# Block attention with a soft mixture of experts: units of 512 tokens by one head pair, quarter-array transposes, v on GpSimd's queue, one arena, full-width w2 and result

## The chip, the cores and the metric

One core of a Trainium2 chip runs the whole program. The metric is device time in microseconds (us) of one execution; three runs of the kernel before are given, and one profiled execution of it. PE is TensorE, DVE is VectorE, ACT is ScalarE, POOL is GpSimd, and SP is the sync engine, which computes nothing here and issues DMAs. A q behind an engine's name means its queue of such instructions.

## The reference, cut to what matters

```python
# attention inside chunks of 64 tokens; B, H, S, D = 8, 8, 576, 64
scores = (q_c @ k_c.T) / sqrt(D)                  # 64 x 64 for each chunk and head
attn = softmax(scores)                            # with 1e-9 in the denominator
x = (attn @ v_c) -> rows of tokens                # N = 4608 tokens, 512 columns: 8 heads of 64
# soft mixture of experts: 8 experts with 4 slots each
logits = x @ phi                                  # 4608 x 32
d = softmax(logits over the tokens);  c = softmax(logits over the slots)
slot_in = d.T @ x                                 # 32 x 512
slot_out[e] = relu(slot_in[e] @ w1[e]) @ w2[e]    # w1: 512 x 1024, w2: 1024 x 512, e = 0..7
out = c @ slot_out                                # 4608 x 512
```

All is float32. The program reads 9.4 MB each of q, k and v and 16.8 MB each of w1 and w2, and writes 9.4 MB.

## The kernel before

**Attention** works on 36 tiles `t` of 128 tokens, that is two chunks of all eight heads. `load_qk` brings 128 tokens of q and of k, with eight tokens of one head (2 KB of DRAM) on each partition; where the two chunks belong to different sequences it takes two DMAs of 1 KB rows each. `load_v` brings v in four DMAs of 64 KB with rows of 256 bytes, from POOL's queue for the first four tiles and from SP's for all others. `transposes` turns q or k with four transposes of the whole 128x128 array (L153, results `pq` and `pk`), and four copies sort each into `qT` and the block-diagonal `kT_bd` (L176 on DVE, L178 on ACT). `s1` makes the scores `psc` (L191) and subtracts the maximum; `s1b` is the exponential; `s2a` transposes the weights (`pt`, L214); `s2b` multiplies by v (`pav`, L231) and divides; `s3` transposes x (`px`, L252). Once in four tiles `logits` (`pl`, L267), `natural` (`pe`) and `partial` (`pp`, L337) carry the softmax over the tokens on.

**Order.** Each engine runs its instructions in the order in which the code issues them; the loop over `t` is written as a software pipeline by hand. One turn of it issues `load_qk(t + 3)`, `load_v(t)`, sometimes a load of 1 MB of w1 (`load_w`), and then on PE: `psc` of tile t, the transposes of t+2, `px` of t-3, `pt` of t-1 and `pav` of t-2. A DMA on SP's queue waits there until its buffer is free, and what stands behind it waits too. There are four buffers for q and k together and three for v.

**Experts.** `up` (`ph`, L549) multiplies the slots by w1, two experts at a time, `turn` transposes the result, and `down` (`po`, L579) multiplies by w2. w2 comes in halves of the columns, in rows of 1 KB: first the left columns of all experts, then the right ones. So the left half of the result can be formed (`pf`, L614, in one-pass float32r with weights that `place_c` has split in two) and written, in rows of 1 KB, while the right columns of w2 still come in.

```python
            if t + 3 < NT:
                load_qk(t + 3)
            load_v(t)
            ...
            s1(t)
            ...
            if t + 2 < NT:
                transposes(t + 2, 1)
                transposes(t + 2, 0)
```

Of the kernel before, what the change touches and what calls it, by code (L numbers as in the profile page):

```python
# [9 lines left out]
F32R = mybir.dt.float32r  # L10
# [6 lines left out]
def kernel(  # L17
# [17 lines left out]
    NC = S // CH                 # chunks per sequence  # L35
# [4 lines left out]
    NT = N // P                  # 128-token tiles, two chunks each  # L40
    PT = P // H                  # partitions per head of a loaded tile
    JT = P // PT                 # tokens per partition of a loaded tile
    J2 = JT // 2
    NL = NT // 4                 # logit batches of four tiles
    E, _, FF = w1.shape
    SL = phi.shape[1]            # slots
# [4 lines left out]
    NWA = 17  # L51
    NWB = 5
    NV = 3
    NQK = 4
    NK = 2

    const = ctx.enter_context(tc.tile_pool(name="const", bufs=1))
    wpa = ctx.enter_context(tc.tile_pool(name="wpa", bufs=NWA))
# [4 lines left out]
    c_all = const.tile([P, NT, SL], F32, name="c_all")  # L63
# [15 lines left out]
    DH = DM // 2  # L79
    wt = {}  # L80
    worder = [(1, e, h) for e in range(E) for h in range(2)]
    worder += [(2, e, h) for h in range(2) for e in range(E)]

    def load_w(pool, n):
        m, e, h = worder[n]
        t = pool.tile([P, 2048], F32, tag="w", name=f"w{m}_{e}_{h}") if pool else qk_w
        if m == 1:
            t = t.rearrange("p (j f) -> p j f", j=2)
            nc.sync.dma_start(t, w1[e].rearrange("(j p) f -> p j f", p=P)[:, 2 * h:2 * h + 2])
        else:  # L90
            t = t.rearrange("p (g f) -> p g f", g=8)
            nc.sync.dma_start(
                t, w2[e].rearrange("(g p) f -> p g f", p=P)[:, :, DH * h:DH * (h + 1)])
        wt[m, e, h] = t

    with ExitStack() as actx:
        ap_ = actx.enter_context(tc.tile_pool(name="attn1", bufs=1))
        asc = actx.enter_context(tc.tile_pool(name="attn_sc", bufs=2))
        av_ = actx.enter_context(tc.tile_pool(name="attn_v", bufs=1))
        a2 = actx.enter_context(tc.tile_pool(name="attn2", bufs=2))  # L100
        ps = actx.enter_context(tc.tile_pool(name="ps", bufs=8, space=PSUM))
# [12 lines left out]
        qTb = [ap_.tile([P, NHP, P], F32, name=f"qT{i}") for i in range(2)]  # L114
        kT_bd = [ap_.tile([P, 2, NHP, P], F32, name="kT_bd0")]
        xT = av_.tile([P, 4, NF, P], F32, name="xT")
        v_bd = [av_.tile([P, 2, NHP, VW], F32, name=f"v_bd{i}") for i in reversed(range(NV))][::-1]
        kT_bd.append(av_.tile([P, 2, NHP, P], F32, name="kT_bd1"))

        def chunk(t, c2):  # L120
            b, c = divmod(2 * t + c2, NC)
            return b, c * CH

        def load_qk(t):
            (b0, s0), (b1, s1_) = chunk(t, 0), chunk(t, 1)
            for src, dst in ((k, qkn[2 * t % NQK]), (q, qkn[(2 * t + 1) % NQK])):
                if b0 == b1:
                    nc.sync.dma_start(
                        dst.rearrange("p j d -> p (j d)"),
                        src[b0][:, s0:s0 + P].rearrange("h (p j) d -> p h (j d)", j=JT),  # L130
                    )
                else:
                    for c2, (b, s0_) in enumerate(((b0, s0), (b1, s1_))):
                        nc.sync.dma_start(
                            dst[:, J2 * c2:J2 * (c2 + 1), :].rearrange("p j d -> p (j d)"),
                            src[b][:, s0_:s0_ + CH].rearrange("h (p j) d -> p h (j d)", j=J2),
                        )

        def load_v(t):
            for c2 in range(2):  # L140
                b, s0 = chunk(t, c2)
                for a in range(2):
                    (nc.gpsimd if t < 4 else nc.sync).dma_start(
                        v_bd[t % NV][CH * a:CH * (a + 1), c2, :, (D + 1) * a:(D + 1) * a + D],
                        v[b, a::2, s0:s0 + CH].rearrange("hp x d -> x hp d"),
                    )

        def transposes(t, isk):
            src = qkn[(2 * t + 1 - isk) % NQK]
            dst = kT_bd[t % NK] if isk else qTb[t % 2]  # L150
            pt = bank(f"p{'qk'[isk]}_{t}")
            for i in range(J2):
                nc.tensor.transpose(  # L153
                    out=pt[:, P * i:P * (i + 1)],
                    in_=src[:, 2 * i:2 * i + 2, :].rearrange("x u d -> x (u d)"),
                    identity=ident,
                )
            pv = pt.rearrange("x (j p hp a) -> x a hp p j", j=J2, a=2, p=PT)
            split = chunk(t, 0)[0] != chunk(t, 1)[0]
            for u in range(2):  # L160
                for a in range(2):
                    r = slice(D * a, D * (a + 1))
                    d = dst[r, a] if isk else dst[r]
                    s = pv[D * u:D * (u + 1), a]
                    pieces = []
                    if not split:
                        pieces.append((d.rearrange("x hp (p j u) -> x u hp p j", j=J2, u=2)[:, u], s))
                    else:
                        J4 = J2 // 2
# [12 lines left out]
        def s1(t):
            psc = bank(f"psc_{t}")
            qT, kb = qTb[t % 2], kT_bd[t % NK]
            for c2 in range(2):
                cs = slice(CH * c2, CH * (c2 + 1))
                for hp2 in range(2):
                    for hpg in range(2):
                        hp = 2 * hpg + hp2
                        o = (c2 * 2 + hp2) * P  # L190
                        nc.tensor.matmul(  # L191
                            psc[CH * hpg:CH * (hpg + 1), o:o + P],
                            lhsT=qT[:, hp, cs],
                            rhs=kb[:, :, hp, cs],
                            start=True, stop=True,
                        )
            pv = psc.rearrange("p (r x) -> p r x", x=CH)
            mx = a2.tile([P, 8], F32, tag="mx", name=f"mx_{t}")
            nc.vector.reduce_max(mx, pv, axis=AX.X)  # L199
            sc = asc.tile([P, 8, CH], F32, tag="sc", name=f"sc_{t}")  # L200
            nc.vector.tensor_tensor(sc, pv, mx.unsqueeze(2).to_broadcast([P, 8, CH]), ALU.subtract)  # L201
            ex[t] = sc

        def s1b(t):
            nc.scalar.activation(ex[t], ex[t], AF.Exp, scale=SCALE)  # L205

        xs = {}
        ats = {}

        def s2a(t):  # L210
            sc = ex.pop(t).rearrange("p (r h) x -> p r (h x)", h=2)
            pt = bank(f"pt_{t}")
            for r in range(4):
                nc.tensor.transpose(out=pt[:, P * r:P * (r + 1)], in_=sc[:, r], identity=ident)  # L214
# [466 lines left out]
```

## Time and profile before

| | |
|---|---|
| three runs | 282.5, 283.17 and 284.31 us, median 283.17 us |
| profiled execution | span 284.7 us from its first to its last instruction; no separate time is given for it |
| PE, DVE, ACT, POOL busy | 236.2, 182.0, 169.6, 20.3 us |
| DMA | 71.83 MB in 77906 packets, mean 252 GB/s; SP's queue 94.3% of 16 engines' span |
| chain that ended last | PE 46%, DMA 42%, DVE 4%, ACT 2% |
| attention | first `psc` at 8.54 us, that of the last tile at 201.10 us |
| experts | first `ph` at 220.63 us |

A profile row gives an engine's busy time in a stretch, or one merged group of instructions with its start, its length and its count. One float32 matmul stands as two records on PE, a transpose as one. DMA share is the mean busy share of the 16 DMA engines; it can exceed 1 since packets overlap.

### The profile page before, as it was taken

The numbers are of one execution on the slowest core, as the hardware profiler recorded it, in microseconds if no ns is written. First come the engines' busy times: TensorE is split into PE (matmuls) and PEld (weight loads), VectorE is DVE, ScalarE is ACT, GpSimd is POOL, SyncE is SP. The second block draws the span as 40 slices with busy tenths as digits, with TensorE's granted clock in tenths as the row PEclk, the third lists the DMA queues.
The fourth block names the chain that finished last, engine by engine and source line by source line (L and its number), as shares of the span: only waits on it lengthen the run. The fifth ranks groups of instructions, "written<-read, shape, count | busy, mean of one in ns | idle before, by whom it ended". The sixth has DMA issues, their size and how long they took to land.

```text
span 284.7 us, 7167 instructions
## 1 busy us (share of the span) xinstructions
PE 236.2 (83%) x2629; PEld 180.3 (63%) x2629; DVE 182.0 (64%) x504; ACT 169.6 (60%) x429; POOL 20.3 (7%) x53
## 2 busy tenths in 40 slices
PE   6869978978798988768997698696899999999850
PEld 3648867767586677557785567575676235677850
DVE  6558838767887797584888378677774402474550
ACT  2778957866767877666786476685642112455440
POOL 8703000000000000000000000000000400000000
PEclk9999979979999999997999799999999999999995
DMA  6998989979989999899999885999979999997797
GB/s 156 210 201 191 255 158 283 267 167 262 271 201 263 270 261 293 183 259 215 265 259 255 145 234 127 282 280 247 210 229 350 341 351 347 348 340 250 263 343 261
DMA packets 77906, 71.83 MB, mean 252 GB/s; under 512 B 37681, under 2 KB 65329, under 8 KB 77873
## 3 DMA queue, kind: packets, MB, share of 16 engines
q1 hardware_dynamic: 77360, 70.34, 94.3%
q0 software_dynamic: 512, 1.05, 1.9%
q8 instruction: 21, 0.34, 0.6%
q14 instruction: 13, 0.10, 0.2%
HBM read 61.93 MB, written 9.44 MB: 251 GB/s over the span
## 4 chain that ended last, share of the span: by engine, by line
PE 46%; DMA 42%; DVE 4%; ACT 2%; issue 1%; SPq 0%; ACTq 0%; DVEq 0%
DMA qk_w<-in_q_dram 29%; DMA qk_w<-in_k_dram 13%; PE pf L614 6%; PE pav L231 6%; PE po L579 5%; PE ph L549 5%; PE pq L153 4%; PE px L252 4%; PE pt L214 3%; PE psc L191 2%; PE pp L337 2%; PE pl L267 2%; PE pk L153 2%; DVE kT_bd L176 1%; PE pc L526 1%
## 5 line engine op out<-in xcount | busy, mean ns | idle before, releaser
L178 ACT COPY qT<-pq 64x256 f32<-64x256 f32 (+1 forms) x160 | 59.6, 385 | 27.8 <-PE pq L153 24.6
L153 PE MATMUL pk<-ident,qk_w 128*128 128x128 f32 x144 | 24.7, 296 | 23.3 <-DMA qk_w<-in_k_dram 19.9
L231 PE MATMUL pav<-v_bd,at 128*64 128x130 f32 x576 | 41.4, 286 | 0.0
L178 ACT COPY kT_bd<-pk 64x256 f32<-64x256 f32 (+1 forms) x76 | 26.8, 365 | 20.3 <-PE pk L153 19.0
L191 PE MATMUL psc<-kT_bd,qT 128*64 128x128 f32 x576 | 38.7, 277 | 0.0
L231 PEld LDWEIGHTS pav<-v_bd,at 128*64 128x64 f32 x576 | 32.4, 140 | 6.4 <-issue 5.0
L176 DVE COPY kT_bd<-pk 64x256 f32<-64x256 f32 (+1 forms) x84 | 33.1, 402 | 5.1 <-PE pk L153 4.2
L153 PEld LDWEIGHTS pk<-ident,qk_w 128*128 128x128 f32 x144 | 15.9, 147 | 31.9 <-issue 18.1
L191 PEld LDWEIGHTS psc<-kT_bd,qT 128*64 128x64 f32 x576 | 33.5, 140 | 0.8 <-issue 0.5
L153 PE MATMUL pq<-ident,qk_w 128*128 128x128 f32 x144 | 25.1, 298 | 9.7 <-DMA qk_w<-in_q_dram 9.6
L241 DVE TENSOR_TENSOR x<-pav,rc 128x256 f32<-128x256 f32 x72 | 27.2, 419 | 1.2
L199 DVE TENSOR_REDUCE mx<-psc 128x8 f32<-128x512 f32 x36 | 24.4, 678 | 4.9 <-PE psc L191 4.9
L153 PEld LDWEIGHTS pq<-ident,qk_w 128*128 128x128 f32 x144 | 17.2, 150 | 15.0 <-issue 5.5
L201 DVE TENSOR_TENSOR sc<-psc,mx 128x512 f32<-128x512 f32 x36 | 24.9, 692 | 2.2
L238 DVE TENSOR_SCALAR rc<-pav 128x4 f32<-128x4 f32 x72 | 10.1, 157 | 24.6 <-PE pav L231 24.3
L252 PE MATMUL px<-ident,x 128*128 128x128 f32 x144 | 23.8, 292 | 0.7 <-DVE x L241 0.7
L214 PE MATMUL pt<-ident,sc 128*128 128x128 f32 x144 | 23.4, 288 | 0.8 <-ACT sc L205 0.8
L205 ACT ACTIVATE sc<-sc 128x512 f32<-128x512 f32 x36 | 23.0, 640 | 0.0
L252 PEld LDWEIGHTS px<-ident,x 128*128 128x128 f32 x144 | 17.3, 148 | 8.7 <-issue 3.7
L216 ACT COPY at<-pt 128x512 f32<-128x512 f32 x36 | 21.2, 589 | 2.7 <-PE pt L214 2.2
L614 PE MATMUL pf<-sst,cst 128*128 128x256 f32 x72 | 18.7, 405 | 0.9 <-DVE sst L601 0.9
L214 PEld LDWEIGHTS pt<-ident,sc 128*128 128x128 f32 x144 | 18.1, 150 | 1.4 <-ACT sc L205 1.0
(97 smaller groups left out, 262.0 us busy)
## 6 DMA issues: line engine op xcount, KB each, us to landing
w<-in_moe_w_dram SPq DMA_DIRECT2D x31, 1024.0 KB, 8.2
out_dram<-ob SPq DMA_DIRECT2D x18, 512.0 KB, 4.6
qk_w<-in_k_dram SPq DMA_DIRECT2D x32, 256.0 KB, 6.3
qk_w<-in_q_dram SPq DMA_DIRECT2D x32, 256.0 KB, 6.2
v_bd<-in_v_dram SPq DMA_DIRECT2D x128, 64.0 KB, 5.3
v_bd<-in_v_dram POOLq DMA_DIRECT2D x16, 64.0 KB, 5.3
qk_w<-in_k_dram SPq DMA_DIRECT2D x8, 128.0 KB, 6.6
qk_w<-in_q_dram SPq DMA_DIRECT2D x8, 128.0 KB, 6.3
```

The lines of the kernel that those rows point to most:

```text
L153: nc.tensor.transpose(out=pt[:, P * i:P * (i + 1)], in_=src[:, 2 * i:2 * i + 2, :].rearrange("x u d -> x (u d)"), identity=ident,)
L176: nc.vector.tensor_copy(o, i_)
L178: nc.scalar.copy(o, i_)
L191: nc.tensor.matmul(psc[CH * hpg:CH * (hpg + 1), o:o + P], lhsT=qT[:, hp, cs], rhs=kb[:, :, hp, cs], start=True, stop=True,)
L199: nc.vector.reduce_max(mx, pv, axis=AX.X)
L201: nc.vector.tensor_tensor(sc, pv, mx.unsqueeze(2).to_broadcast([P, 8, CH]), ALU.subtract)
L205: nc.scalar.activation(ex[t], ex[t], AF.Exp, scale=SCALE)
L214: nc.tensor.transpose(out=pt[:, P * r:P * (r + 1)], in_=sc[:, r], identity=ident)
L231: nc.tensor.matmul(pav[CH * c2:CH * (c2 + 1), hp2 * VW:(hp2 + 1) * VW], lhsT=at[:, 2 * c2 + hp2, hpg, :], rhs=v_bd[t % NV][:, c2, 2 * hpg ...
L241: nc.vector.tensor_tensor(x.rearrange("p (b h d) -> p b h d", b=2, d=D)[:, hpg], av[hpg][:, :, 0:D], rc[:, hpg].to_broadcast([P, 4, D]), A ...
L252: nc.tensor.transpose(out=px[:, P * f:P * (f + 1)], in_=xs[t][:, P * f:P * (f + 1)], identity=ident)
L614: nc.tensor.matmul(pf[:, DH * j:DH * (j + 1)], lhsT=cv[:, 2 * j2 + j, :], rhs=sst[h], start=True, stop=True)
```

## The change

The work is cut the other way. A unit `u` is now 512 tokens of one head pair (36 units again, with the same number of bytes and scores). Each engine's code is issued in much the same hand-written order. What differs:

- `load_qk` puts four tokens of one head (1 KB) on a partition, two heads side by side. Where the 512 tokens cross a sequence's end, in 28 of the 36 units, q and k take two DMAs each. The loads run four units ahead and have three buffers each for q and k.
- `transposes` uses 32 matmuls by a quarter of the identity, each 64x64 on one quarter of the array, for q and k together; one ACT copy sorts q, two sort k. DVE's part in them is gone, and `s3`'s copy is always DVE's.
- `load_v` is on POOL's queue for all units, two DMAs for a unit, or four where it is cut.
- `logits` runs for every unit, a quarter as much at a time.
- PSUM is held by three pools (3 single banks, 1 for `pl` and `po`, 2 double banks) in place of one of eight.
- All big buffers are slices of one `arena`. w2 comes by half an expert in rows of 8 KB (`places` says where); six of its 16 loads are issued at the end of the attention, the other ten after `up` has left w1's slots.
- `down` runs once, 512 columns wide; the result is formed in two-pass float32 matmuls with 32 rows each (`turned`, `combine`), after all of `down`, and written in rows of 2 KB.

```diff
-    NQK = 4
+    NQK = 3
+    places = list(range(NW1)) + [18, 19, 20, 17, 21, 22] + list(range(10))
...
+            nc.sync.dma_start(t, w2[e, DM * h:DM * (h + 1)].rearrange("(p r) f -> p (r f)", r=4))
...
+    def load_qk(u):
+        b, hp = divmod(u, NHP)
+        for i, src in enumerate((k, q)):
+            dst = nat[2 * (u % NQK) + i]
+            for g, n, sq, s0 in pieces(b, JT):
+                nc.sync.dma_start(
+                    dst[g:g + n].rearrange("g a j d -> g a (j d)"),
+                    src[sq, 2 * hp:2 * hp + 2, s0:s0 + JT * n].rearrange("a (g j) d -> g a (j d)", j=JT),
+                )
...
+    def load_v(u):
+        b, hp = divmod(u, NHP)
+        for a in range(2):
+            for c, n, sq, s0 in pieces(b, CH):
+                nc.gpsimd.dma_start(
+                    v_bd[u % NV][CH * a:CH * (a + 1), c:c + n, (D + 1) * a:(D + 1) * a + D],
+                    v[sq, 2 * hp + a, s0:s0 + CH * n].rearrange("(c x) d -> x c d", x=CH),
+                )
...
+    def transposes(u):
+        pt = two_banks(f"pqk_{u}")
+        for i in range(2):
+            src = nat[2 * (u % NQK) + 1 - i]
+            for j in range(JT):
                 for a in range(2):
+                    for s in range(2):
+                        rs = slice(64 * s, 64 * (s + 1))
+                        o = 64 * (JT * i + j)
+                        nc.tensor.matmul(pt[D * a:D * (a + 1), s, o:o + 64], lhsT=src[rs, a, j, :],
+                                         rhs=ident[rs, rs], start=True, stop=True)
+        pv = pt.rearrange("x s (i j g) -> x i s j g", i=2, j=JT)
+        nc.scalar.copy(qTb[u % 2].rearrange("x (s g j) -> x s j g", s=2, j=JT), pv[:, 0])
+        for a in range(2):
+            r = slice(D * a, D * (a + 1))
+            nc.scalar.copy(kT_bd[u % 2][r, a].rearrange("x (s g j) -> x s j g", s=2, j=JT), pv[r, 1])
...
+        if t + 4 < NU:
+            load_qk(t + 4)
+        if t > 0:
             load_v(t)
...
         s1(t)
+        if t >= 4:
+            logits(t - 4)
...
+        transposes(t + 2)
...
+    def combine(b):
+        ob = at_(oplaces[b], 0, SLOT).rearrange("p (j f) -> p j f", j=4)
+        pair = [two_banks(f"pf_{b}_{i}") for i in range(2)]
+        pf = [pair[j // 2][:, j % 2] for j in range(4)]
+        for j in range(4):
+            nc.tensor.matmul(pf[j], lhsT=c_all[SL * j:SL * (j + 1), b], rhs=sst[SL * j:SL * (j + 1)],
+                             start=True, stop=True)
...
     for e in range(0, E, 2):
         hrs[e] = up(e)
+        for _ in range(min(4, len(worder) - nw)):
+            load_w()
...
+        down(e)
+    spread()
+    for b in range(NB):
+        combine(b)
```

PE, one turn of the loop that has no work of a whole batch, before (`psc` scores, `pk` and `pq` transposes of k and q, `px`, `pt`, `pav` as above):

```order
L191 MATMUL psc_1190<-kT_bd_97,qT_95 64x128 x8
L153 MATMUL pk_1203<-ident,qk_w 128x128 x4
L153 MATMUL pq_1212<-ident,qk_w 128x128 x4
L252 MATMUL px_1221<-ident,x_1167 128x128 x4
L214 MATMUL pt_1227<-ident,sc_1133 128x128 x4
L231 MATMUL pav_0_1237<-v_bd_101,at_1164 64x130 x4
L231 MATMUL pav_1_1243<-v_bd_101,at_1164 64x130 x4
```

The same turn after the change (`pqk` holds both q and k):

```order
L178 MATMUL psc_1792<-arena 64x128 x8
L232 MATMUL pl_1616<-arena,phi_sb 32x128 x4
L164 MATMUL pqk_1808<-ident,arena 64x64 x32
L220 MATMUL px_1844<-ident,arena 128x128 x4
L193 MATMUL pt_1850<-ident,arena 128x128 x4
L202 MATMUL pav_1857<-arena 64x130 x8
```

Eight transposes became 32 matmuls at the same place, and `pl` comes in every turn; the rest keeps its place.

SP, two turns in the middle of the attention, before:

```order
L128 DMA qk_w<-in_k_dram 128x1x512
L128 DMA qk_w<-in_q_dram 128x1x512
L143 DMA v_bd_100<-in_v_dram 64x4x64 x4
L89 DMA w_5_0_1848<-in_moe_w_dram 128x2x1024
L128 DMA qk_w<-in_k_dram 128x1x512
L128 DMA qk_w<-in_q_dram 128x1x512
L143 DMA v_bd_99<-in_v_dram 64x4x64 x4
```

SP, two turns at about the same place, after:

```order
L139 DMA arena<-in_k_dram 80x2x256
L139 DMA arena<-in_k_dram 48x2x256
L139 DMA arena<-in_q_dram 80x2x256
L139 DMA arena<-in_q_dram 48x2x256
L111 DMA arena<-in_moe_w_dram 128x2x1024
L139 DMA arena<-in_k_dram 80x2x256
L139 DMA arena<-in_k_dram 48x2x256
L139 DMA arena<-in_q_dram 80x2x256
L139 DMA arena<-in_q_dram 48x2x256
```

The four loads of v have left SP, and q and k take two DMAs each here. On POOL there now stand, where only one multiplication for each batch stood:

```order
L148 DMA arena<-in_v_dram 64x3x64
L148 DMA arena<-in_v_dram 64x5x64
L148 DMA arena<-in_v_dram 64x3x64
L148 DMA arena<-in_v_dram 64x5x64
L294 TENSOR_TENSOR c_all<-c_all,cs_1309 128x128
L148 DMA arena<-in_v_dram 64x3x64
L148 DMA arena<-in_v_dram 64x5x64
```

So each unit has four (or two) loads of v on POOL, and that multiplication, which waits for DVE, stands between them once in four units.

More of the change, by code (lines that the diff above doesn't have):

```diff
@@ L34 @@
     CH = 64
-    NC = S // CH
     NHP = H // 2
@@ new lines, in warm, with pieces @@
+    def warm(n, src=ident):
+        pd = bank("pd")
+        for _ in range(n):
+            nc.tensor.matmul(pd[:, 0:src.shape[1]], lhsT=src[:, 0:P], rhs=src, start=True, stop=True)
+    def pieces(b, n):
+        out_ = []
+        t = 512 * b
+        while t < 512 * (b + 1):
+            e = min(512 * (b + 1), (t // S + 1) * S)
+            out_.append(((t - 512 * b) // n, (e - t) // n, t // S, t % S))
+            t = e
+        return out_
+    def load_qk(u):
[7 more added lines that the diff above has]
+                )
@@ new lines, in s3, with logits @@
+    def s3(u):
+        b, hp = divmod(u, NHP)
+        px = bank(f"px_{u}")
+        for r in range(4):
+            nc.tensor.transpose(out=px[:, P * r:P * (r + 1)],
+                                in_=xbuf[b % 2][:, r, P * hp:P * (hp + 1)], identity=ident)
+        nc.vector.tensor_copy(xTb[u % 2], px)
+    pls = {}
+    lst = {}
+    def logits(u):
+        b, hp = divmod(u, NHP)
+        if hp == 0:
+            pls[b] = psl.tile([P, 512], F32, tag="pl", name=f"pl_{b}")
+        for r in range(4):
+            nc.tensor.matmul(pls[b][SL * r:SL * (r + 1), 0:P], lhsT=phi_sb[:, hp, :],
+                             rhs=xTb[u % 2][:, P * r:P * (r + 1)], start=(hp == 0), stop=(hp == NHP - 1))
@@ new lines, in slots @@
+    def slots(wsel, ws):
+        for j in range(4):
+            pst = bank(f"pst_{j}")
+            nc.tensor.matmul(pst[:, 0:SL], lhsT=p_run[:, P * j:P * (j + 1)], rhs=wsel, start=True, stop=True)
+            nc.scalar.copy(siT[:, j, :], pst[:, 0:SL])
+        pn = bank("pn")
+        nc.tensor.matmul(pn[:, 0:1], lhsT=rep.rearrange("p g s -> p (g s)"), rhs=ws, start=True, stop=True)
+        nc.vector.tensor_scalar_add(rden, pn[:, 0:1], EPS)
+        nc.vector.reciprocal(rden, rden)
+    load_qk(0)
@@ new lines @@
+    load_v(L - 1)
+    while nw < NW1:
+        load_w()
+    s1(L - 1)
+    logits(L - 5)
+    s2a(L - 2)
+    s1b(L - 1)
+    s1(L)
+    for _ in range(3):
+        load_w()
+    s3(L - 4)
+    s2b(L - 3)
+    load_v(L)
+    s2a(L - 1)
+    s1b(L)
+    logits(L - 4)
+    weights(NB - 2)
+    sums(NB - 2)
+    s2b(L - 2)
+    s2a(L)
+    s3(L - 3)
+    s2b(L - 1)
+    natural(NB - 2, False)
+    logits(L - 3)
+    s2b(L)
+    s3(L - 2)
+    partial(NB - 2)
+    load_w()
+    s3(L - 1)
+    logits(L - 2)
@@ new lines @@
+    s3(L)
+    logits(L - 1)
+    for _ in range(2):
+        load_w()
+    warm(1)
+    logits(L)
+    weights(NB - 1)
+    shifted(NB - 2)
+    warm(2)
+    wmin = lane_minimum()
+    natural(NB - 1, False)
+    wj = lane_weights(*wmin)
+    sums(NB - 1)
+    warm(1)
+    ss = lane_select(wj)
+    partial(NB - 1)
+    shifted(NB - 1)
+    warm(3)
+    slots(*ss)
+    combination(NB - 2)
+    combination(NB - 1)
+    hzs = [at_(23, 8 * SL * e, 8 * SL).rearrange("p (g s) -> p g s", s=SL) for e in range(E)]
```

702 lines of the change are left out of this document (232 added, 470 removed).

## Prediction

> **What bounds the kernel now.** I read the stages first, then short stretches with one kind of transfer, then SP's order, then a stretch in which PE never waits. The stages (windows; the last three columns are granted clock, DMA share and GB/s):
>
> ```profile
> 50.00:100.00 50.00, 42.82 (x521) 34.84 (x520) 37.76 (x108) 37.01 (x95) 0.80 (x2) 0.97 1.00 243
> 100.00:150.00 50.00, 42.51 (x516) 35.01 (x516) 37.45 (x103) 35.64 (x95) 1.20 (x3) 0.97 1.02 247
> 150.00:200.00 50.00, 38.47 (x464) 31.12 (x464) 35.27 (x103) 32.85 (x85) 0.80 (x2) 0.97 0.95 224
> ```
>
> The DMA engines hold a packet nearly all the time and yet move only 224 to 247 GB/s. Stretches with one kind alone: v from SP, w1 (rows of 4 KB), q and k (2 KB), w2 (1 KB), the result (1 KB), in this order:
>
> ```profile
> 62.50:64.50 2.00, 2.00 (x20) 2.00 (x22) 0.23 (x2) 1.93 (x6) 0.00 (x0) 0.50 0.46 105
> 84.00:86.00 2.00, 2.00 (x34) 1.83 (x33) 0.83 (x4) 1.88 (x6) 0.00 (x0) 1.00 1.00 406
> 3.00:5.00 2.00, 1.30 (x5) 0.72 (x4) 1.06 (x3) 0.00 (x0) 1.81 (x8) 1.00 1.05 255
> 216.00:222.00 6.00, 5.32 (x47) 3.28 (x50) 3.97 (x19) 2.30 (x12) 0.19 (x1) 1.00 1.09 349
> 276.00:282.00 6.00, 0.00 (x0) 0.00 (x0) 0.00 (x0) 0.00 (x0) 0.00 (x0) 0.51 1.04 345
> ```
>
> v moves at 105 GB/s with the engines 46% busy. SP's timeline there:
>
> ```profile
> 60.91 2.62 SPq L143 DMA_DIRECT2D v_bd<-in_v_dram  x4
> 63.58 0.60 SPq L89 DMA_DIRECT2D w<-in_moe_w_dram  x1
> 64.28 0.56 SPq L128 DMA_DIRECT2D qk_w<-in_k_dram  x1
> 64.93 0.55 SPq L128 DMA_DIRECT2D qk_w<-in_q_dram  x1
> ```
>
> Issuing v takes SP 2.62 us, in which the engines get little else. With q, k and half a w1 load, SP needs 2.62 + 0.55 + 0.56 + 0.30 = 4.0 us a tile for issue alone. PE's timeline, two turns without a wait (the first has `pl` and `pe`, the second `pp`):
>
> ```profile
> 133.54 1.04 PE L191 MATMUL psc<-kT_bd,qT 128*64 128x128 f32 x16
> 134.51 1.08 PE L267 MATMUL pl<-xT,phi_sb 128*32 128x128 f32 x32
> 135.52 0.66 PE L153 MATMUL pk<-ident,qk_w 128*128 128x128 f32 x4
> ...
> 137.36 0.33 PE L305 MATMUL pe<-ident,eT 128*128 128x128 f32 x1
> ...
> 137.77 1.18 PE L231 MATMUL pav<-v_bd,at 128*64 128x130 f32 x16
> 138.71 1.11 PE L191 MATMUL psc<-kT_bd,qT 128*64 128x128 f32 x16
> 139.76 0.66 PE L153 MATMUL pk<-ident,qk_w 128*128 128x128 f32 x4
> 140.25 0.60 PE L153 MATMUL pq<-ident,qk_w 128*128 128x128 f32 x4
> 140.78 1.06 PE L337 MATMUL pp<-x,eN 128*32 128x512 f32 x8
> 141.78 0.69 PE L252 MATMUL px<-ident,x 128*128 128x128 f32 x4
> 142.31 0.60 PE L214 MATMUL pt<-ident,sc 128*128 128x128 f32 x4
> 142.84 1.11 PE L231 MATMUL pav<-v_bd,at 128*64 128x130 f32 x16
> 143.78 1.04 PE L191 MATMUL psc<-kT_bd,qT 128*64 128x128 f32 x16
> ```
>
> From start to start the turns last 5.17 and 5.07 us; without `pp` (1.00) the second is 4.07. Four turns, one of each and two plain, need (5.17 + 5.07 + 2 x 4.07) / 4 = 4.60 us each. What a tile really takes follows from the first and the last tile's scores:
>
> ```profile
> 8.54 1.75 PE L191 MATMUL psc<-kT_bd,qT 128*64 128x128 f32 x16
> 201.10 1.09 PE L191 MATMUL psc<-kT_bd,qT 128*64 128x128 f32 x16
> ```
>
> (201.10 - 8.54) / 35 = **5.50 us a tile**, 0.9 above PE's need. So transfers and their issue lead the attention, with PE close behind. From 201.1 on it is 83.6 us to the end of the span, nearly all at the DMA rates of 349 and 345.
>
> **The attention, part by part.** DMA first; a unit has 0.524 MB of q and k, 0.262 MB of v, and on average 16.8 / 35 = 0.48 MB of w1.
> - w1 stays: 0.48 MB at 406 GB/s, 1.18 us.
> - q and k, now rows of 1 KB: no row shows such loads of theirs alone. Ends: 255 GB/s as their 2 KB rows now, 2.06 us; 349 as w2's 1 KB rows, 1.50 us. I take 2.06, the same tensors.
> - v by POOL. The queue table and v's own line have the four tiles that use that queue today:
>
> ```profile
> q0 software_dynamic: 512, 1.05, 1.9%
> L143 SPq DMA_DIRECT2D v_bd<-in_v_dram x128: 595/607/2156, 25.9 to 206.4; - x128
> L143 POOL DMA_DIRECT2D v_bd<-in_v_dram x16: 615/617/780, 5.3 to 24.2; - x16
> ```
>
> 1.9% of 284.7 us is 5.4 us for four tiles, 1.35 a unit; the other end is SP's share, 0.46 x 2.5 us = 1.16. I take 1.35. POOL needs 4 x 0.617 = 2.5 us of issue a unit and has nothing else but the one multiplication in four units, which waits for DVE at the end of a turn; the next v load has to wait for that turn's `pav` anyway.
>
> Sum for DMA: 1.18 + 2.06 + 1.35 = 4.59 us a unit (3.84 by the lower ends). SP issues four loads of q and k and half a w1 load, 4.5 x 0.6 = 2.7 us: hidden. With three buffers instead of two, q and k are asked for a turn earlier, so a single late load costs less.
>
> The Trainium skill ("DMA: Bandwidth & Descriptors", Issuing engines are not separate DMA queues) says against this that issuing from several engines saves only the sequencer's time, which it calls usually small beside the DMA. Here it is 2.62 us a tile at a share of 0.46, so not small; by the rule the turn would stay as it is, which is rival B below.
>
> PE next. `pqk` replaces `pk` and `pq` (0.49 + 0.44). No instruction of this trace uses half of the rows, so it must be bounded. It is 32 matmuls, 64 records of 64 columns. `psc`'s 16 records of 128 columns need 0.87 us, two strips of the array at a time: 109 ns for 128 columns, 54 for 64. Four quarters at a time: 64 x 54 / 4 = 0.87 us. Two at a time: 1.74. One: 3.5. That column strips start independently is in the windows of `pl` alone, four records begun within 30 ns, four more 0.14 us later:
>
> ```profile
> 134.55:134.58 0.03, 0.03 (x4) 0.03 (x8) 0.00 (x0) 0.00 (x0) 1.00 0.33 137
> 134.69:134.72 0.03, 0.03 (x8) 0.03 (x4) 0.00 (x0) 0.00 (x0) 1.00 0.99 410
> 219.62 0.81 PE pst L378 x8
> ```
>
> And `pst` (the chain's row), 128 weight columns with only 32 streamed, takes 101 ns a record, so 64 weight columns load in about 51, under the 54. I take four at a time, by the nearest row, `pl`. A change of shape costs about 0.13 us: `psc` lasts 0.97 and 1.05 from start to start for 0.87 of streaming. So `pqk` 1.00, `pl` for each unit a quarter of 1.01 plus 0.13 = 0.38, `psc` 0.97, `px` 0.53, `pt` 0.53, `pav` 0.94, and a quarter of `pp` (1.00) and `pe` (0.41), 0.35: **4.70 us** a unit (3.70 without `pqk`).
>
> The Trainium skill ("TensorEngine Tiling (Array Packing)", Performance Considerations) puts about 60 cycles of overhead on each matmul, so that one with few columns gains nothing. By that, and the 2.4 GHz that the Trainium skill gives ("Trainium Kernel Development and Optimization", NeuronCore Architecture), 64 records would be an estimate of 1.6 us, near rival A; here the `pl` windows show four records begun in 30 ns, so no such overhead is paid one after the other.
>
> ACT loses half its copies of q and k: three of the kind of `at` (589 ns) instead of six or so of 0.4; DVE loses 33.1 us of L176 and takes over all of `xT`. Both stay below 4 us a unit, hidden under PE.
>
> ```profile
> L216 ACT COPY at<-pt 128x512 f32<-128x512 f32 x36 | 21.2, 589 | 2.7 <-PE pt L214 2.2
> L620 DVE COPY ob<-pf 128x512 f32<-128x512 f32 x18 | 12.2, 689 | 4.0 <-PE pf L614 3.9
> ```
>
> PE's 4.70 and DMA's 4.59 lie so close that neither hides the other's stalls; between 4.70 and today's 5.50 I take **5.0 us**. Last scores: 8.5 + 35 x 5.0 = 183.5 us, 17.6 earlier.
>
> **The tail, counted from the last scores.** Rows for it:
>
> ```profile
> 220.63 7.00 PE ph L549 x64
> 0.74 0.69 SPq L128 DMA_DIRECT2D qk_w<-in_k_dram  x1
> 4.24 1.09 PE L153 MATMUL pk<-ident,qk_w 128*128 128x128 f32 x4 [0.70 <-DMA qk_w<-in_k_dram]
> ```
>
> - To the first `ph`: 220.63 - 201.10 = 19.5 now; about 1.0 more for `pl` in six groups instead of three. 20.5.
> - Half of 7.00 for the first `up`: 24.0. The six early w2 loads (6.3 MB, 15.5 us) lie under it, but the DMA engines then run dry, since the other ten wait for w1's slots.
> - A load's first bytes: 4.24 - 0.74 less 1.03 us of data, 2.4. Ten loads, 10.5 MB: with rows of 8 KB the nearest row is w1's 406 GB/s, 25.8 us (30.0 at 349). 52.2.
> - The last eight `po` records 0.9, the gather on DVE 0.7, spreading 0.9, its copy 0.6, hand-overs 0.2: 55.5.
> - First pair of the result 1.0, copy 0.7, issue and first bytes 2.0: 59.2. These 7 us, in which nothing is transferred, are new: today the left half of the result is written while w2 comes in.
> - 9.44 MB at 345 GB/s, 27.4 us (23.3 at 406), and 1.8 as now from the last packets near 282.9 to the span's end: **88.4**. Ends: 84 and 93.
>
> Sum: 183.5 + 88.4 = 271.9 of span. The median of the runs, 283.17, lies 1.5 below the profiled span of 284.7, so **270 us**, 4.6% faster. Every 0.1 us of the turn is 3.5 us; the change breaks even at a turn of 5.37.
>
> **Rivals.**
> - A, slower: halves of the rows do not run side by side. Then `pqk` is 1.87 with its change of shape, the turn 5.57, and `combine`, four strips of 32 rows with 72 records of 512 columns (about 0.44 each), takes 31 us instead of a quarter of that, over the 27.4 of the writes. 8.5 + 195 + 88.4 + 4 - 1.5 = 294. It decides once `pqk` is over about 1.6. For it: no row shows row strips. Against: the independent column strips. One quarter at a time would give about 350.
> - B, no change: DMA stays the bound, because q and k by 1 KB and v by another queue are served no faster together, at a turn of 5.4: 8.5 + 189 + 88.4 - 1.5 = 284. For it: the share of 1.00 in the stages. Against: 105 GB/s at 0.46.
> - C, faster: the turn falls to PE's need and the result's 2 KB rows run like w1's: 8.5 + 164.5 + 84.3 - 1.5 = 256.
> - D: the wide w2 does not do what its rows suggest and comes at 349: 274, inside my case's range.
>
> **How the numbers follow.** My case, turns of 4.8 to 5.2 with a tail of 86 to 91, 260 to 278: 0.58 with D. A 0.15, one quarter at a time or a starved v 0.04, B 0.14, C 0.09. The range runs from 257 to 295: it takes in A and B and leaves out the 0.04 above and about half of C. About 1% is what a measurement of this kernel can tell from no change. Faster by more than that: 0.58 + 0.09 + 0.02 of B, 0.69; within: 0.12; slower: 0.19.
>
> **What the profile after would show.** Right: scores each 5.0 us, `pqk` near 0.9 us for 64 records, few waits of PE for q and k, DMA above 260 GB/s in the attention, a hole of about 7 us in DMA between w2 and the result, w2 near 400 GB/s. Wrong: `pqk` of 1.7 or more; PE waiting for `v_bd`; a DMA share of 1 at 245 GB/s as now; copies on ACT longer than 0.6 us, since one instruction now sorts 512 columns.

## The result, and the profile after

| | before | after |
|---|---|---|
| time, median | 283.74 us (282.5 to 286.23, 4 runs) | 314.45 us (311.82 to 318.2, 4 runs) |
| ratio to before, 95% interval | | **1.103** (1.094 to 1.112): slower |
| profiled span | 284.7 us | 310.0 us (forecast 271.9) |
| first and last scores | 8.54 and 201.10 | 10.19 and 213.92 |
| turn | 5.50 us | 5.82 us (forecast 5.0) |
| tail behind the last scores | 83.6 us | 96.1 us (forecast 88.4) |

The miss of 38.1 us is 1.7 at the start, 35 x 0.82 = 28.7 in the turns, and 7.7 in the tail. (The ratios leave out executions more than 1.5% above the fastest of their kernel; the profiles of x3 and x4 are of such executions, and from them only single stages and kinds of waits are read.)

The page of after: the chain by engine, the groups that the change made, the instruction queue's row.

```profile
PE 55%; ACT 20%; DVE 10%; issue 9%; DMA 4%; SPq 0%; POOL 0%; ACTq 0%; DVEq 0%
...
L170 ACT COPY arena<-pqk 64x512 f32<-64x512 f32 x72 | 80.5, 1118 | 0.9
L167 ACT COPY arena<-pqk 128x512 f32<-128x512 f32 x36 | 39.6, 1101 | 41.3 <-PE pqk L164 41.1
L164 PE MATMUL pqk<-ident,arena 64*64 64x64 f32 x2304 | 47.6, 234 | 17.3 <-issue 11.3
...
q8 instruction: 36, 0.59, 0.9%
```

The chain now runs over PE and ACT, hardly over transfers, and 9% of it, 28 us, is "issue": an engine that waits for nothing the profile shows. The three ACT copies last 1.10 to 1.12 us, not 0.589. The windows of the three stages quoted of before (same columns):

```profile
50.00:100.00 50.00, 43.38 (x919) 34.92 (x918) 29.02 (x73) 35.55 (x50) 21.42 (x34) 0.91 0.86 226
100.00:150.00 50.00, 41.50 (x926) 33.08 (x926) 29.66 (x76) 38.86 (x59) 21.53 (x35) 0.97 1.01 222
150.00:200.00 50.00, 42.22 (x932) 33.99 (x932) 29.12 (x74) 35.84 (x53) 21.44 (x34) 0.96 0.92 227
```

PE has 920 to 930 records per 50 us instead of 464 to 521, and the transfers fall to 222 to 227 GB/s, partly at a share of 0.86. PE's timeline shows where an "issue" stall sits:

```profile
141.78 0.50 PE L178 MATMUL psc<-arena 128*64 128x128 f32 x6
142.20 0.43 PE L232 MATMUL pl<-xT,phi_sb 128*32 128x128 f32 x8
142.65 0.57 PE L164 MATMUL pqk<-ident,arena 64*64 64x64 f32 x23
146.69 0.83 PE L164 MATMUL pqk<-ident,arena 64*64 64x64 f32 x41 [3.47 <-issue]
```

PE stops for 3.47 us between the 23rd and the 24th of 64 records of one group, whose operands had all been there: no semaphore is waited for in the middle. Otherwise 64 records take 1.1 us.

Three theories: **C**, the long copies make ACT (5.0 us a unit) the bound; **F**, PE is not supplied with instructions in time; **D**, the transfers are the bound all along (rival B of the prediction; these letters are not those of the prediction's rivals). For F speaks a constant: PE has 4,506 matmul and 4,506 weight records, 36 instruction packets, 250 records each; before it was 2 x 2,629 and 21 packets, 250 each. The times of the packets in the trace say the same: the one that moved during the stall above ended at 145.23 us, 1.46 us before PE went on. PE has 11 stalls of this kind that last more than 0.6 us, 19.5 us together, and each ends 1.3 to 1.6 us after the end of an instruction packet, though these packets come 4 to 20 us apart.

### The profile page after: what moved, and what is told of

Its sections match the earlier page's. It is cut to its first block, busy times and chain, and to the rows that moved or that the text cites. A ratio compares the mean times of both kernels' runs of the same rounds, so it can differ in the third digit from the quotient of the medians.

```text
span 310.0 us, 10574 instructions
## 1 busy us (share of the span) xinstructions
PE 253.2 (82%) x4506; PEld 174.7 (56%) x4506; DVE 149.3 (48%) x374; ACT 180.3 (58%) x271; POOL 93.3 (30%) x158
## 3 DMA queue, kind: packets, MB, share of 16 engines
q0 software_dynamic: 5120, 9.45, 14.4%
## 4 chain that ended last, share of the span: by engine, by line
PE 55%; ACT 20%; DVE 10%; issue 9%; DMA 4%; SPq 0%; POOL 0%; ACTq 0%; DVEq 0%
PE pqk L164 10%; ACT arena L170 9%; PE pav L202 8%; PE psc L178 6%; PE pf L518 5%; PE ph L467 5%; PE px L220 5%; ACT arena L167 5%; PE po L496 4%; PE pt L193 4%; DMA arena<-in_v_dram 2%; PE pl L232 2%; DVE arena L525 2%; DMA arena<-in_q_dram 2%; PE pp L306 2%
## 5 line engine op out<-in xcount | busy, mean ns | idle before, releaser
L148 POOL DMA_DIRECT2D arena<-in_v_dram x128 | 83.5, 660 | 82.4 <-PE pav L202 66.2
L170 ACT COPY arena<-pqk 64x512 f32<-64x512 f32 x72 | 80.5, 1118 | 0.9
L167 ACT COPY arena<-pqk 128x512 f32<-128x512 f32 x36 | 39.6, 1101 | 41.3 <-PE pqk L164 41.1
L164 PE MATMUL pqk<-ident,arena 64*64 64x64 f32 x2304 | 47.6, 234 | 17.3 <-issue 11.3
L164 PEld LDWEIGHTS pqk<-ident,arena 64*64 64x64 f32 x2304 | 41.5, 146 | 27.8 <-issue 15.7
L202 PE MATMUL pav<-arena 128*64 128x130 f32 x576 | 42.8, 289 | 5.4 <-DMA arena<-in_v_dram 3.2
L178 PE MATMUL psc<-arena 128*64 128x128 f32 x576 | 40.6, 282 | 5.0 <-issue 5.0
L202 PEld LDWEIGHTS pav<-arena 128*64 128x64 f32 x576 | 33.1, 141 | 12.5 <-issue 11.5
L178 PEld LDWEIGHTS psc<-arena 128*64 128x64 f32 x576 | 34.7, 142 | 6.1 <-issue 5.8
L209 DVE TENSOR_TENSOR arena<-pav,rc 128x256 f32<-128x256 f32 x72 | 27.1, 418 | 1.2
L183 DVE TENSOR_TENSOR arena<-psc,mx 128x512 f32<-128x512 f32 x36 | 24.9, 692 | 2.2
```

Source lines behind the costliest of these rows:

```text
L148: nc.gpsimd.dma_start(v_bd[u % NV][CH * a:CH * (a + 1), c:c + n, (D + 1) * a:(D + 1) * a + D], v[sq, 2 * hp + a, s0:s0 + CH * n].rearrange ...
L164: nc.tensor.matmul(pt[D * a:D * (a + 1), s, o:o + 64], lhsT=src[rs, a, j, :], rhs=ident[rs, rs], start=True, stop=True)
L167: nc.scalar.copy(qTb[u % 2].rearrange("x (s g j) -> x s j g", s=2, j=JT), pv[:, 0])
L170: nc.scalar.copy(kT_bd[u % 2][r, a].rearrange("x (s g j) -> x s j g", s=2, j=JT), pv[r, 1])
L178: nc.tensor.matmul(psc[CH * c2:CH * (c2 + 1), P * r:P * (r + 1)], lhsT=qT[:, cs], rhs=kb[:, :, cs], start=True, stop=True)
L183: nc.vector.tensor_tensor(scb[u % 2].rearrange("p (r x) -> p r x", x=CH), pv, mx.unsqueeze(2).to_broadcast([P, 8, CH]), ALU.subtract)
```

## The experiments

The edits are shown shortened.

**x1, copies in the order of the destination.** PSUM is read with a stride, SBUF written without gaps.

```
- nc.scalar.copy(qTb[u % 2].rearrange("x (s g j) -> x s j g", s=2, j=JT), pv[:, 0])
+ pg = pt.rearrange("x s (i j g) -> x i s g j", i=2, j=JT)
+ nc.scalar.copy(qTb[u % 2].rearrange("x (s g j) -> x s g j", s=2, j=JT), pg[:, 0])   # kT_bd likewise
```

> The changed kernel with its three ACT copies of a unit's transposes walking in the order of the destination: PSUM is read with a stride of 64 floats, SBUF is written without gaps. The result is unchanged. Theory C (copies): the scattered write of 16-byte steps is what makes a copy of 512 columns 1.11 us instead of 0.585, and ACT with 5.0 us a unit is on the path of nearly every turn. Then the copies come down to about 0.6 us, ACT to 3.4 us a unit, the turn from 5.82 to about 5.2 and the time from 314 to about 292. If the price is the reading side, the copies stay at 1.1 us or grow, and so does the time. Theory F (PE's own instruction supply): copies get shorter, but the turn stays within 0.15 us of 5.82, 309 to 314 us. Theory D (DMA is the bound): copies get shorter, the time stays within 1% of 314.

312.79 us, ratio to before 1.098 (1.078 to 1.118). The copies, and the chain:

```profile
L168 ACT COPY arena<-pqk 128x512 f32<-128x512 f32 x36 | 21.1, 586 | 68.4 <-PE pqk L164 68.3
...
L171 ACT COPY arena<-pqk 64x512 f32<-64x512 f32 x72 | 41.8, 580 | 0.9
...
PE 75%; issue 10%; DMA 5%; DVE 4%; ACT 3%; SPq 0%; POOL 0%; ACTq 0%; DVEq 0%
```

The scattered write is the price of the copy (1.11 to 0.58 us), but the time stays: ACT leaves the chain, issue does not, and PE's stalls of more than 0.6 us now add up to 27.5 us instead of 19.5. C alone is not the cause; whether the copies would count without the stalls, x1 can't tell (y3 can).

**x2, 8 transposes of 128x128 a unit instead of 32 of 64x64**, 16 records for 64. **x3**, both edits.

```
- nc.tensor.matmul(pt[D * a:D * (a + 1), s, o:o + 64], lhsT=src[rs, a, j, :], rhs=ident[rs, rs], ...)   # 4 per j
+ jj, a = divmod(j, 2)
+ nc.tensor.transpose(out=pt[:, i, P * j:P * (j + 1)], in_=src[:, a, 2 * jj:2 * jj + 2, :] (as 128 columns), identity=ident)
```

> The changed kernel with 8 transposes of 128x128 a unit instead of 32 of 64x64: 16 records of PE instead of 64, about the same streaming time (two transposes of today's kind lasted 0.49 and 0.44 us for four). It leaves out the right placing of the heads: q and k of a pair lie mixed, everything else is as before. Theory F: PE's streams of records are long enough that fetching instructions stalls it (issue stalls of 1.3 to 3.7 us, 9% of the span on the chain); with 1,728 of 4,506 records gone the issue share of the chain falls below 4% and the time from 314 to about 290 to 297. Theory C: ACT's copies are as long as before, the turn stays 5.6 to 5.9, the time 307 to 315. Theory D: within 1% of 314.

> Both edits together: copies in the order of the destination and 8 transposes a unit instead of 32 (q and k of a pair lie mixed, as in the run with 8 transposes alone). If C and F are two parts of one loss, each hidden partly under the other, this falls by more than either alone: turn 4.9 to 5.1, 280 to 287 us. If C alone holds, it equals the run with the copies; if F alone, the run with 8 transposes. Theory D: over 308.

x2: 297.98 us, 1.039 (1.021 to 1.057). x3: 296.59 us, 1.031 (1.016 to 1.046). x2's chain, instruction row and last scores:

```profile
PE 40%; DMA 28%; ACT 20%; DVE 6%; issue 2%; SPq 1%; POOL 0%; ACTq 0%
...
q8 instruction: 20, 0.33, 0.5%
...
196.44 1.09 PE L175 MATMUL psc<-arena 128*64 128x128 f32 x16
```

With 20 packets instead of 36 issue falls from 9% to 2% and the last scores come 17.5 us earlier, with the copies still at 1.11 us; no such stall of more than 0.6 us is left. Shorter copies on top (x3) bring nothing that can be measured; x3's chain is half DMA waits. F carries some 17 us; what is left lies on transfers and copies (28% and 20% of x2's chain).

**y3, the changed kernel without the loads of q, k, v after the third unit**: same instructions of PE, little to transfer.

> The changed kernel without the loads of q, k and v after the third unit (old data is used again); w1 still comes, and every instruction of PE, ACT and DVE stays. Theory F1 (PE's instructions are fetched by packets that have to wait among the data packets): with the engines mostly idle the issue stalls go, the issue share of the chain falls from 9% below 3%, and the turn falls to ACT's need of 5.0 us: last scores near 187 us, 282 to 286 in all. Theory F2 (64 short records outrun the supply of instructions whatever else is moved): issue stays at 8 to 10%, the turn at 5.5 to 5.8, 300 to 310 us.

289.6 us (one run), last scores at 196.27. Within this one run both conditions occur. Windows while w1 still comes in and after that, then PE's waits in the second stretch:

```profile
14.00:42.00 28.00, 20.11 (x513) 16.96 (x514) 12.45 (x26) 22.89 (x27) 0.00 (x0) 1.00 1.03 385
50.00:190.00 140.00, 126.97 (x2974) 100.80 (x2966) 92.86 (x240) 117.63 (x171) 2.41 (x6) 1.00 0.07 25
...
PE pt L193 <- DVE arena L183: 5.9, 6, 1.0
PE pqk L164 <- ACT arena L170: 3.7, 6, 0.6
PE pe L267 <- ACT eT L247: 1.0, 6, 0.2
PE pqk L164 <- issue: 1.0, 1, 1.0
```

```profile
20.36 0.80 PE L164 MATMUL pqk<-ident,arena 64*64 64x64 f32 x39
23.43 0.58 PE L164 MATMUL pqk<-ident,arena 64*64 64x64 f32 x25 [2.27 <-issue]
```

At a DMA share of 1.03 PE stalls inside its groups as in after; at 0.07 one stall of 1.0 us is left in 140 us. F1 holds: with the engines full of data an instruction packet comes too late, and 250 records, which PE uses up in one to two turns, are too few to cover that. Where the packet waits the traces do not show. The total came out 4 us above what was expected, since the turn is not ACT's 5.0 even where the stalls and the transfers are gone. First and last scores of four turns that recur from batch to batch in y3, in x2 and in r1 (below, with short copies and 16 records), and y3's chain from 50 to 190 us:

```profile
107.06 1.04 PE L178 MATMUL psc<-arena 128*64 128x128 f32 x16
128.59 1.04 PE L178 MATMUL psc<-arena 128*64 128x128 f32 x16
...
150.00 1.04 PE L175 MATMUL psc<-arena 128*64 128x128 f32 x16
171.17 1.04 PE L175 MATMUL psc<-arena 128*64 128x128 f32 x16
...
107.40 1.04 PE L176 MATMUL psc<-arena 128*64 128x128 f32 x16
126.86 1.04 PE L176 MATMUL psc<-arena 128*64 128x128 f32 x16
...
by line: ACT arena L170 17.5%; PE pqk L164 11.4%; PE pav L202 10.5%; ACT arena L167 9.0%; DVE arena L209 6.5%; DVE arena L183 6.0%; PE pt L193 5.2%; DVE mx L182 5.2%; PE psc L178 5.0%; issue 4.5%; PE px L220 3.4%; ACT arena L194 2.5%; PE pl
```

Per turn that is 5.38 us in y3, 5.29 in x2 and 4.87 in r1. In y3 the long copies (L167 and L170) hold 26.5% of the chain. So C is real too, some 0.4 us a turn between x2 and r1 (x2 also loads v); it does not show in x1 and x3 because there the stalls or the transfers set the turn.

**x4, combine alone**: ACT and DVE empty different double banks, every second batch uses other banks.

```
- pf = [pair[j // 2][:, j % 2] for j in range(4)]
+ even b: pf = [pair[i][:, x] for x in range(2) for i in range(2)];  odd b: three of bank(...), one of psl
```

> The changed kernel with only combine altered: ACT empties one double bank and DVE the other, and every second batch uses the four other banks, so that DVE does not wait for ACT's copy and PE does not wait for the batch just before. Theory L (lockstep): a batch takes 3.49 us because 2.10 of PE, 0.59 of ACT and 0.70 of DVE follow each other; freed of that the last stage is bound by the writes, 3.04 us a batch by the 345 GB/s of before, and the time falls by 4 to 6 us to about 309. Rival: PE at half its clock with records of 1.02 us, or the writes themselves, set the 3.49 us; then it stays within 1 us of 314.

310.20 us, 1.083 (1.065 to 1.102). One batch in after's chain, from batch to batch 3.49 us:

```profile
287.20 2.10 PE pf L518 x6
289.33 0.59 ACT arena L523
289.95 0.70 DVE arena L525
290.69 2.10 PE pf L518 x6
```

DVE's copy starts when ACT's of the same double bank ends, though it reads another bank. In x4 the stage from the first `pf` to the end lasts 29.9 us instead of 34.8, as expected.

**y1, the kernel before with v by GpSimd throughout**, the part that the prediction counted on; **y4**, x3 with v by SP; **y2**, x3 with q and k in rows of 2 KB (8 tokens a row, partition 2 g + a).

```
y1: - (nc.gpsimd if t < 4 else nc.sync).dma_start(      + nc.gpsimd.dma_start(
y4: - nc.gpsimd.dma_start(                              + nc.sync.dma_start(
y2: - "a (g j) d -> g a (j d)", j=JT                    + j=2 * JT
```

> The kernel before with one part of the change alone: v by GpSimd's queue for all tiles instead of the first four. The prediction's theory (v from SP costs 2.62 us of issue a tile, in which the engines are 46% busy): the turn falls from 5.50 to about 4.9, 284 to about 263 to 268 us. Rival B (DMA stays the bound; what v's packets and q's, k's and w1's take adds up to the same 5.3 to 5.5 us whoever issues): within 1.5% of 284. Software-made packets could also be dearer: then slower, 290 or more.

> As the run with both edits, but v issued by SP again, four DMAs a unit with rows of 256 bytes as GpSimd issues them. The prediction's theory: SP then needs 2.7 + 4 x 0.6 = 5.1 us of issue a unit beside the engines' time; the turn goes up from 5.43 to 5.6 or more, the time from 296 to 302 or more. Rival B: the engines are full either way, and who issues v changes nothing: within 1% of 296.

> As the run with both edits (copies in the order of the destination, 8 transposes a unit, DMA waits on 52% of its chain), but q and k come in rows of 2 KB (8 tokens) instead of 1 KB; number of DMAs, transposes and copies unchanged. It leaves out the right placing of tokens and heads. Theory R (row size): the engines are full at 233 to 238 GB/s because a row of 1 KB takes longer per byte than one of 2 KB; the turn falls from 5.43 to about 5.0, the time from 296 to about 281. Rival: the size of the rows does not matter at this load, time within 1% of 296; then the software queue or w1's rows make the engines full.

y1: 291.73 us (285.5 to 296.3; before 281.7 to 284.6 beside it), in the fastest execution scores from 8.38 to 198.10, a turn of 5.42: no gain. y4: 308.82 us, 1.092 (1.084 to 1.100), 6% above x3 by the ratios: in the new form it does matter who issues v, and SPq takes 9% of the chain. But v from SP also comes in smaller packets (71,501 in all, 37,710 in x3), so SP's issue is not shown to be the whole price. y2: 304.44 us, 1.079 (1.071 to 1.087): row size R falls, the turn is 5.45; why it is slower than x3 stays open.

**Transfers by themselves**: of after (d_after), of before (d_before), of after without v (d_no_v); no arithmetic, 9.4 MB written behind them.

> Only the transfers of the changed kernel's attention, in its order, with its buffers and from its queues (q and k in rows of 1 KB and w1 from SP, v from GpSimd), then 9.4 MB written to the result; all arithmetic and the experts are left out. It measures the disputed DMA need of a unit by itself: 45 MB for 36 units. The prediction's sum (4.59 us a unit, low end 3.84): the loads end after 140 to 170 us. Rival B (the mix cannot be moved faster than 235 to 245 GB/s, whatever PE does): 185 to 195 us, as in the full kernels.

> Only the transfers of the attention of the kernel before, in its order, with its buffers and queues (q and k in rows of 2 KB, v and w1, all from SP), then 9.4 MB written to the result; all arithmetic and the experts are left out. SP's issue is 4.0 us a tile. The prediction's reading (SP's issue of v costs time that no transfer uses): the loads take the most of 4.0 us of issue and the transfers that do not fit under it, 5.0 to 5.5 us a tile, 180 to 195 us, clearly longer than the changed kernel's transfers alone. Rival B: both take the same, 185 to 195 us.

> Only the transfers of the changed kernel's attention, as in the run of transfers alone (q, k and w1 done after 177 us), but without v after the first unit; all arithmetic and the experts are left out. 35.9 MB. If v costs its share of bytes or the 1.35 us a unit that the prediction took, the loads end after 128 to 140 us; if v's pieces of 256 bytes cost 1.8 us or more a unit, after 105 to 118 us (320 to 340 GB/s).

Spans in this order, and 60 to 120 us of d_after and d_no_v (the last three columns are clock, share, GB/s):

```profile
span 201.8 us, 369 instructions
span 212.9 us, 348 instructions
span 149.7 us, 238 instructions
...
60.00:120.00 60.00, 0.00 (x0) 38.38 (x61) 1.00 1.08 243
60.00:120.00 60.00, 0.00 (x0) 0.00 (x0) 1.00 1.08 308
```

Less some 25 us of writes (9.4 MB at 380 to 408 GB/s) that is 4.9 us a unit for after and, less 5 more for the 2 MB of w2 that before also loads, 5.1 for before: the change saves the engines 0.2 us a unit, not 0.9. v costs (201.8 - 149.7) / 35 = 1.49 us a unit; the rest runs at 308 GB/s without it, all at 243 with it. That lies between the two prices that were expected of v, nearer to the prediction's 1.35.

**r1, x3 without v after the third unit.**

> As the run with both edits (copies in the order of the destination, 8 transposes a unit), without the loads of v after the third unit (old data is used again; heads lie mixed as there). If v's software-made packets are what makes the engines full (they hold 20 to 22% of the engines' time for 18% of the bytes), the rest fits under PE and the turn falls from 5.43 to the engines' own 4.85 to 4.95, with a DMA share near 0.85: last scores near 182 us, 275 to 279 in all. If q, k and w1 are the bound by themselves, the share stays at 1 and the turn above 5.2.

264.91 us (one run):

```profile
11.30 1.98 PE L176 MATMUL psc<-arena 128*64 128x128 f32 x16
171.87 1.09 PE L176 MATMUL psc<-arena 128*64 128x128 f32 x16
...
50.00:100.00 50.00, 47.58 (x606) 38.92 (x604) 37.47 (x97) 30.14 (x65) 1.20 (x3) 1.00 0.75 227
```

A turn of 4.59, PE busy 95%, share 0.75: without v the transfers fit under PE, and PE's need, with 16 records for the transposes and short copies, is near the 4.70 of the forecast.

**z1, the causes taken away, result unchanged**: 8 transposes in two single banks and eight copies of 64x256, single banks for `pav` and `pf`, `s2b(L - 3)` and `load_v(L)` right behind `s1(L - 1)`. **z2, z3**: besides, four and six of the sixteen w1 loads behind the last q and k. **b1**: the kernel before with four of its w1 loads there.

```
z1: + s1(L - 1); s2b(L - 3); load_v(L); ...          pf = [bank(f"pf_{b}_{j}") for j in range(4)]
z2: - while nw < min(NW1, NW1 * (t - 1) // (NU - 7)):
    + while nw < min(NW1 - 4, (NW1 - 4) * (t - 1) // (NU - 7)):
b1: - while nw < min(NWA, NWA * (t - 2) // (NT - 6)):    + NWA - 4 for NWA, the other four behind load_v(t - 1)
```

> The changed kernel with the causes found so far taken away and the result unchanged: 8 transposes of 128x128 a unit instead of 32 of 64x64 (16 records of PE instead of 64), eight copies of 64x256 in the order of the destination instead of three (k's on DVE in every fourth unit), single PSUM banks, so that combine's copies on ACT and DVE do not wait for each other, and the last unit's v loaded two steps earlier. If instruction supply, combine's lockstep and the late v are the whole loss, what is left is a DMA-bound turn of 5.35 to 5.45, last scores at 200 us, a tail of 86 to 88: 285 to 290 us, about as the kernel before. If something else of the change costs time (arena, wide w2), it stays above 295.

> As the repaired kernel, but four of the sixteen w1 loads (4.2 MB) are issued behind the last loads of q and k instead of between them. The result is unchanged. Theory B (DMA need of the mix is the bound of the attention): 0.12 MB less a unit at 235 to 243 GB/s is 0.5 us, the turn falls from 5.36 to about 4.9, the last scores from 198.5 to about 182; in the tail the four loads take 10 us at 406 GB/s, of which all but 2 to 4 us lie under the slots' computation, where the engines are half idle. 268 to 274 us. If the turn is bound by something else (order of buffers, PE, ACT), it stays above 5.25 and the time at 282 to 288.

> The same with six of the sixteen w1 loads behind the last q and k. Theory B: 0.18 MB less a unit, 0.75 us; the engines' own turn (4.6 to 4.9, as without v) takes over as the bound, last scores at 173 to 178; the tail gets 3 to 6 us longer than with four, since w2 then comes in behind 6.3 MB of w1. 266 to 274 us, within 3 us of the run with four. If the turn does not follow the bytes: 282 to 290.

> The kernel before with the same edit alone: four of its w1 loads behind the last q and k. The result is unchanged. Theory B: the turn falls from 5.50 to 5.0 (SP's issue, 4.0 us, stays under it), last scores near 184; its tail is bound by transfers of 1 KB rows at 345 to 349 GB/s, so the 4.2 MB are paid there in full, 10 to 12 us: 276 to 281 us. If SP's issue of v is what holds the attention, as the prediction had it, the turn falls only by the 0.07 us of issue: 284 to 294 us.

z1: 284.64 us, ratio 1.001 (0.995 to 1.008): level with before. z2: **274.89 us, 0.969 (0.962 to 0.976)**, faster than both kernels: its four executions (273.87 to 275.86) lie below all seven of before beside them (282.2 to 289.25). z3: 276.19, 0.977 (0.969 to 0.986), no better: its turn of 4.95 is near the engines' own, for z2 and z3 both repeat the same four turns, about 4.2, 5.1, 5.2 and 6.6 us, once the batches run. Both came out 1 to 2 us above the range expected. b1: 288.45, 1.016 (1.007 to 1.025), 7 us above it. Last scores of z1, z2 and b1:

```profile
198.52 1.09 PE L175 MATMUL psc<-arena 128*64 128x128 f32 x16
186.38 1.09 PE L175 MATMUL psc<-arena 128*64 128x128 f32 x16
186.74 1.09 PE L191 MATMUL psc<-kT_bd,qT 128*64 128x128 f32 x16
```

Turns of 5.36, 5.02 and 5.09 (b1: 5.50 before). The turn follows the bytes in both forms, by 0.34 and 0.41 where 0.5 was expected; SP issues v in b1 as ever, so its issue did not hold the attention. What b1 wins there (14.4 us) it pays in its tail, 97.9 instead of 83.6 us, more than the 10 to 12 expected. All of it lies ahead of the first `ph` (33.8 us after the last scores instead of 19.5), and most of it is one wait for the last tile's v, whose loads stand on SP's queue behind the w1 loads that were moved:

```profile
194.69 6.84 SPq L143 DMA_DIRECT2D v_bd<-in_v_dram  x4
...
206.76 2.68 PE L231 MATMUL pav<-v_bd,at 128*64 128x130 f32 x16 [12.12 <-DMA v_bd<-in_v_dram]
```

So b1 paid for its order, not for the 1 KB rows of w2 as was expected. In z2, where v comes from POOL and the last one earlier, the tail grows from 84.5 to 86.6 only.

## Why the prediction was wrong

**The turn, 5.0 predicted, 5.82 measured.** Three steps failed, and since each by itself leads to a turn of 5.3 or more, taking away one gains little. The first is the sum for PE, "64 x 54 / 4 = 0.87 us": it counts what the records take on the array and nothing for bringing 1.7 times the records to PE. The 64 records do last 1.1 us, four quarters at a time, so rival A is refuted. But at the change from one instruction packet to the next PE stalls while the DMA engines are busy (after and y3's first 40 us against the rest of y3, and x2). The stalls add up to 19.5 us, 0.56 a turn; x2's turn of 5.29 is 0.53 lower.

The second step that failed is "transfers and their issue lead the attention", from 105 GB/s at a share of 0.46 in two microseconds while SP issued v. Over 50 us the share was 1.00 all the same, by the prediction's own first rows: the engines worked off elsewhere what they missed there. y1 and b1 show that this issue was not the bound; rival B was right for the attention, with 0.14 put on it. The rule that it cited, the Trainium skill ("DMA: Bandwidth & Descriptors", Issuing engines are not separate DMA queues), agrees with y1 (5.42 for 5.50 us). In y4 moving v back to SP goes with a loss of 6%, part of which may be the smaller packets.

The sum of 4.59 us for DMA was low: 4.9 alone (d_after). Its v was nearly right (1.35; 1.49). The 406 GB/s of w1 and the 255 of q and k came from stretches with one kind alone; together they run at 308, with v at 243. In z1, with no stall left and DMA in the chain, the turn is 5.36; why the transfers need more beside the arithmetic than alone is not shown.

PE's need itself, 4.70, was near with 16 records: 4.59 in r1 over all turns, and 4.87 in its later ones (4.16, 4.16, 5.16 and 5.98 from scores to scores, again and again).

**ACT, "three of the kind of `at` (589 ns)", "hidden under PE".** This is the third step. Measured 1.11, which the prediction's list of signs had named. It did not stay hidden: with hardly a transfer and one stall the turn of the changed form is 5.38 (y3), 5.29 with 16 records (x2), against r1's 4.87. By these turns the change would have come out close to its break-even turn of 5.37 even without the other two faults. x1 and x3, where shorter copies bring nothing, show only that another bound was then as high. The Trainium skill ("SBUF — State Buffer", Door 1: The DMA port swizzle) says that SBUF is accessed in lines of 16 bytes, and that an access pattern which goes to a new line with each element pays for it. The copy writes every 16 bytes, so by that sentence a price could have been foreseen, not its size. The trace agrees: 1.11 us with that write, 0.58 without gaps, 0.39 for 256 elements 8 bytes apart (z1).

**The tail, 88.4 predicted, 96.1 measured.** To the first `ph` 24.9 instead of 20.5: the last unit's v, which waits for a buffer, came late.

```profile
216.94 1.35 POOL L148 DMA_DIRECT2D arena<-in_v_dram  x2 [4.34 <-PE pav L202]
225.35 1.55 PE L202 MATMUL pav<-arena 128*64 128x130 f32 x16 [3.23 <-DMA arena<-in_v_dram]
...
238.86 3.64 PE L467 MATMUL ph<-arena,siT 128*32 128x512 f32 x32
258.64 13.94 PE L496 MATMUL po<-arena 128*32 128x512 f32 x128
275.26 1.14 PE L518 MATMUL pf<-arena,c_all 32*128 32x512 f32 x8 [0.68 <-ACT arena L508]
```

Without that load (y3) it is 20.1, with it two steps earlier (z1) 19.9, as forecast. From there to the end of `po` the forecast had the w2 loads as the bound; PE was, with 33.7 us. The stage of the result took 34.8 instead of 32.9, by the lockstep of x4. The rates were at least what was taken: w2 came at 421 to 426 GB/s for 406 (the prediction's rival D is out), the result at 380 in z1 for 345.

```profile
GB/s 188 254 153 253 253 217 243 171 248 265 248 127 261 252 157 239 222 267 194 254 247 204 248 256 263 77 171 90 286 71 338 297 426 421 214 18 358 303 284 257
```

The last eight slices of 7.75 us also show the hole that was forecast (18). z2's tail takes 4.2 MB more of w1 for 2 us. That b1's takes them for 14 is no measure of the wide w2, since 12 of those are the wait for the last v; what w2 in rows of 1 KB would cost in z2 was not tested.

## What to carry over

A rate of one kind of transfer alone says little of a mix: where the share of the DMA engines is 1 over tens of microseconds, sum the bytes of the mix at the mix's rate, and look for gains in what can be moved to a stage with idle engines, as z2 did, but put nothing that is needed soon behind it on the same queue, as b1 did. Where several bounds lie close together, an edit that removes one shows little; a run without the transfers (y3) showed what the engines need by themselves. Before splitting one instruction into four, count the records that the engine will run per microsecond while the DMA engines are full. In this program a double bank that two engines empty ties their copies together; single banks don't.

## What was not expected of the hardware

- PE's instructions arrive during the run in packets of 16 KB, one for about 250 matmul and weight records (36, 21 and 20 packets for 9,012, 5,258 and 4,980 records). With full DMA engines a stall at such a place lasted up to 3.5 us; with idle ones there was next to none. The stalls end 1.3 to 1.6 us after the end of a packet (after). The kernels with 5,258 and 4,980 records (before and x2) have no such stall of more than 0.6 us, though their DMA share is as high.
- Four row strips of 32 do run side by side: in z1 combine's 72 records of 512 columns took 10.85 us in one piece, 0.15 each.
- Loading v in pieces of 256 bytes lowers the rate of the whole mix: q, k and w1 at 308 GB/s without it, 243 GB/s in all with it, at a DMA share of 1.08 in both.
